# One over the sums on the values instead of the probabilities: eight blocks of attention instead of four

## The chip, the cores and the metric

The program runs on one core of one Trainium2 chip. A core has five engines, each with its own queue of instructions that it works through in order: TensorE (PE in the profile; PEld is its weight load) multiplies matrices, VectorE (DVE), ScalarE (ACT) and GpSimd (POOL) work element by element, and SyncE (SP) here only issues DMA transfers. The queues wait for each other by semaphores. What is measured is the time of one execution in microseconds (us). The median of three runs of the kernel before is 627.17 us (624.49, 627.32 and 627.17).

## The reference

Three layers follow one another. First comes an attention over q, k and v of 2 batches, 8 heads, 768 tokens and 64 features, in which a token sees itself, the 127 tokens before it and the first four of its batch:

```python
keep = is_sink | ((rel >= 0) & (rel < window))          # 4 sinks, window 128
scores = np.where(keep, scale * q @ k.T, -1e9)
a = np.exp(scores - scores.max(-1, keepdims=True))
a = a / (np.sum(a, axis=-1, keepdims=True) + 1e-09)
x = a @ v                                               # -> 1536 x 512
```

Then a gated layer, `silu(x @ w_gate) * (x @ w_val) @ w_out`, with weights of 512 x 1536 and 1536 x 512 that arrive as 64-bit floats. Last, a token with `x @ w_skip > 0` is sent to the one of eight experts that `x @ w_gate` ranks first, and the expert's `relu(x @ w1) @ w2`, times its probability, is added to x. The output is 1536 x 512 in float32.

## The kernel before

The 1536 tokens are 12 blocks of 128, six for each batch, and a block's eight heads are four pairs. Four blocks are a group (`GS = 4`). The gated layer takes the 1536 hidden columns in 12 chunks for one group at a time (`mlp(ph)`); a chunk is a projection with w_gate, one with w_val (`proj`, line 502) and, one chunk later, the product with w_out (`down`, line 514). All large products are made of three: high part times high part, high times low, low times high (`act_copy` makes a high part, `lo_of` subtracts it to get the low one; line 70 and line 73 are these two helpers).

The attention is a generator, `attention()`, that issues its work in pieces: `step_a` turns q and k of a pair (`tqk`), `step_b` makes the scores (`s`, line 296), applies the mask and finds the maximum on VectorE (line 312), and takes the exponential on ScalarE, which sums at the same time (line 316). `step_d` turns the probabilities (`tpt`, line 342), ScalarE copies them out (`pt`), and GpSimd zeroes what the mask excludes. `step_s` turns the probabilities of the sinks. `step_e`, once a block, multiplies the turned probabilities by the values (`xps`, lines 378 and 395) and splits the result into the high and low part `xt` that the projections read. Blocks 0 to 3 run alone; then the first pass of the gated layer begins (the first group, from about 67 to 208 us), and blocks 4 to 7 are issued in the gaps between its pieces, in proportion. Blocks 8 to 11 run in the second pass in the same way.

How the probabilities are divided by their sums depends on the block. For blocks below `LATE_SUM` the sums of all heads are kept in one tile (lines 305 to 308) and inverted once per block (line 325). In `step_e` eight matmuls spread the inverses into a PSUM tile `rps` (line 386: each takes one column of the inverses as a broadcast weight, against the unit matrix, 16 passes of 64 rows in the trace), ScalarE copies it to `rs` (line 388), VectorE multiplies the weighted values by it (line 401), and high and low part are made from the product. For the other blocks each pair inverts its two sums (lines 280 and 281), VectorE scales the probabilities of one head (line 323) and ScalarE those of the other (line 321).

While the first pass runs, its weights come in 36 pieces of 512 KB through three staging buffers (`st`). ScalarE and VectorE convert each piece in two instructions each (lines 136 and 137, then 141 and 142), and `prep` splits it into high part on ScalarE and low part on GpSimd (`ring`). In the same pass the rows of the experts' scratch in DRAM are cleared (`clear_rows`): eight transfers (line 602) from one zeroed tile (`trash`). That tile, `rs`, and some later tiles share one pool of four buffers (`"x2"`).

In PSUM, a pool of two buffers (`attp`) serves the attention of blocks 4 to 11: `tqk`, `s`, `tpt`, `tsk` and `xps` take turns in it. Another one of two (`gvp`) serves the projections, and for blocks 0 to 3 `tpt` and `rps`. Which instruction stands where on an engine's queue is set before the run by a scheduler that follows the order of issue, the priorities and when buffers come free.

Of the kernel before, what the change touches and what calls it, by code (L numbers as in the profile page):

```python
# [8 lines left out]
F32 = mybir.dt.float32  # L9
# [6 lines left out]
P = 128  # L16

@with_exitstack
def build(ctx: ExitStack, tc: tile.TileContext, q, k, v, n_sink, window,
# [5 lines left out]
    NPAIR = H // 2  # L25
# [6 lines left out]
    GS = 4  # L32
    FIRST = list(range(0, NB_ALL + 1, GS))
    GB = 2

    LATE_SUM = 4
    PHASES = [(0, 0, GS, 0, NFC, 2 * GS), (1, 0, GS, 0, NFC, 3 * GS)]
    PHASES += [(2, 0, GB, 0, NFC, 3 * GS), (2, GB, GS, 0, NFC, 3 * GS)]
    XT_SLOT = [0, 1, 0]
# [21 lines left out]
    gvp = fast.enter_context(tc.tile_pool(name="gvp", bufs=2, space=PSUM))  # L61
    attp = fast.enter_context(tc.tile_pool(name="attp", bufs=2, space=PSUM))
# [3 lines left out]
    att = early.enter_context(tc.tile_pool(name="att", bufs=1))  # L66
    sm = early.enter_context(tc.tile_pool(name="sm", bufs=2))

    def act_copy(out, in_, scale=1.0):
        nc.scalar.activation(out=out, in_=in_, func=ACTF.Copy, scale=scale)  # L70

    def lo_of(out, in_, hi, eng=None):
        (eng or nc.vector).tensor_tensor(out=out, in0=in_, in1=hi.bitcast(F32), op=ALU.subtract)  # L73
# [205 lines left out]
    def invert(s):  # L279
        nc.vector.tensor_scalar(out=s, in0=s, scalar1=1e-9, scalar2=None, op0=ALU.add)  # L280
        nc.vector.reciprocal(out=s, in_=s)

    def step_b(j):
# [20 lines left out]
        st = sm.tile([P, 4], F32, tag="st", name="st", bufs=3)  # L304
        if n < LATE_SUM:
            if pr == 0:
# [8 lines left out]
        for h in range(2):  # L315
            nc.scalar.activation(out=p[:, h], in_=p[:, h], func=ACTF.Exp, scale=-1.0, bias=st[:, h:h + 1], accum_out=su[:, h:h + 1])  # L316
        if n >= LATE_SUM:
            invert(su)
# [47 lines left out]
    def new_xt(slot, shape):  # L366
        return [xtp.tile(shape, F32R, tag=f"xt{a}{slot}", name=f"xt{a}") for a in range(2)]

    def step_e(n):

        b, i = divmod(n, NBLK)
        g = [n >= f for f in FIRST].index(False) - 1
        u = n - FIRST[g]
        x = (acqp if n < GS else attp).tile([P, NPAIR, P], F32, tag="acq" if n < GS else "att", name="xps")
        sk = skt.pop(n)

        for pr in range(NPAIR):
            nc.tensor.matmul(out=x[:, pr], lhsT=vsk[b][:, 2 * pr:2 * pr + 2, :].rearrange("p h d -> p (h d)"), rhs=sk,
                             start=pr == 0, stop=False, skip_group_check=True)
        if n < LATE_SUM:  # L380

            r = gvp.tile([P, NPAIR, P], F32, tag="gv", name="rps")
            inv = sums.pop(n)
            for pr in range(NPAIR):
                for h in range(2):
                    nc.tensor.matmul(out=r[64 * h:64 * h + 64, pr], lhsT=inv[:, 2 * pr + h:2 * pr + h + 1].to_broadcast([P, D]), rhs=ident, start=True, stop=True, skip_group_check=True)
            rs = mo.tile([P, RW], F32, tag="x2", name="rs", bufs=4)[:, 0:DM].rearrange("p (a f) -> p a f", a=NPAIR)
            act_copy(rs, r)
        last = 0 if i == 0 else 1
        for pr in range(NPAIR):  # L390
            d = pt.pop(NPAIR * n + pr)
            for s in range(last + 1):
                vv = vb[n - s]
                for h in range(2):
                    nc.tensor.matmul(out=x[64 * h:64 * h + 64, pr], lhsT=vv[:, 2 * pr + h, :], rhs=d[:, s, h],
                                     start=False, stop=s == last and pr == NPAIR - 1, skip_group_check=True)
        if u == 0:
            xt[g] = new_xt(XT_SLOT[g], [P, KD, NG])
        hi, lo = (xt[g][a][:, :, u * P:(u + 1) * P] for a in range(2))
        if n < LATE_SUM:  # L400
            nc.vector.tensor_tensor(out=rs, in0=x, in1=rs, op=ALU.mult)
            x = rs
        act_copy(hi, x)
        lo_of(lo, x, hi)
# [3 lines left out]
    def attention():  # L408
# [8 lines left out]
        for j in range(NP_ALL):  # L417
# [16 lines left out]
            if pr == 0 and n > 0 and n != GS:  # L434
                step_e(n - 1)
                done = n
                if n % NBLK == 0:
                    load_sinks(n // NBLK)
                yield done
            step_d(j)  # L440
            yield done
            if pr == NPAIR - 1:
                step_s(n)
                yield done
                if n == GS - 1:
                    step_e(n)
                    done = n + 1
                    yield done
        step_e(NB_ALL - 1)
        yield NB_ALL  # L450

# [801 lines left out]
```

## Time and profile before

| | |
|---|---|
| median of 3 runs | 627.17 us |
| profiled execution | 628.91 us, of which the span on the core is 627.2 |
| TensorE busy | 592.5 us (94%), mean granted clock 0.988 |
| VectorE busy | 443.4 us (71%) |
| ScalarE busy | 368.3 us (59%) |
| GpSimd busy | 192.1 us (31%) |

The profile is of one execution. TensorE is busy nearly the whole time, so what counts is where it is not, and what is added to its queue. "Busy" of TensorE is the time from the first to the last of its matmuls in flight. The granted clock is what share of full speed TensorE had. Idle time of another engine costs nothing by itself.

### The profile page before, as it was taken

Reading aid. Unit: us, or ns where it says so; the run is one execution under the profiler, and the core shown is the slowest. Engines: PE = TensorE matmul, PEld = TensorE weight load, DVE = VectorE, ACT = ScalarE, POOL = GpSimd, SP = SyncE. Lnnn points to the kernel's source line nnn. Section 1 sums busy time; section 2 is a strip of 40 time slices with the busy share of each in tenths; the row PEclk is TensorE's granted clock in tenths of the full one; section 3 lists DMA queues with packets and bytes.
Section 4 is the critical chain, followed back from the end, with each engine's and each line's share of the span. In section 5 each row is a group of like instructions: output and inputs, shape, how many; then the busy total and the mean of one; then the engine's idle time right before and its main releaser. Section 6 shows DMA issues by size and latency. Waiting matters only on the chain. (4 is left out here: it accounts for less than half of the span.)

```text
span 627.2 us, 10713 instructions
## 1 busy us (share of the span) xinstructions
PE 592.5 (94%) x3459; PEld 472.1 (75%) x3459; DVE 443.4 (71%) x1092; ACT 368.3 (59%) x863; POOL 192.1 (31%) x275
## 2 busy tenths in 40 slices
PE   5899998989999999999999999999998999999993
PEld 3566766667777878777778999899986777787772
DVE  3778889797546485665654577778748696989961
ACT  4699776876545355545543456657526675866740
POOL 2465352666343041101111030021005343526411
PEclk9999999989999999999999999999997999999998
DMA  8745879554010220100004200023107886968901
GB/s 201 166 142 154 244 243 271 184 169 101 1 34 1 85 52 18 33 15 4 1 1 152 101 30 2 0 67 111 36 35 229 284 262 212 331 210 286 322 9 38
DMA packets 78421, 75.83 MB, mean 121 GB/s; under 512 B 43138, under 2 KB 55426, under 8 KB 78352
## 3 DMA queue, kind: packets, MB, share of 16 engines
q1 hardware_dynamic: 75552, 69.32, 36.9%
q0 software_dynamic: 2512, 5.68, 2.7%
q8 instruction: 32, 0.52, 0.3%
q14 instruction: 37, 0.30, 0.2%
q10 hardware_dynamic: 288, 0.00, 0.0%
HBM read 65.37 MB, written 11.98 MB: 123 GB/s over the span
## 5 line engine op out<-in xcount | busy, mean ns | idle before, releaser
L502 PE MATMUL gv<-xt,ring 128*128 128x512 f32 (+1 forms) x1152 | 226.6, 346 | 0.4 <-DVE th L536 0.4
L502 PEld LDWEIGHTS gv<-xt,ring 128*128 128x128 f32 x1152 | 176.8, 190 | 27.4 <-issue 2.0
L70 ACT ACTIVATE ring<-w 128x512 fp32r<-128x512 f32 x144 | 90.2, 629 | 98.5 <-PE gv L502 72.1
L73 DVE TENSOR_TENSOR ring<-w,ring 128x512 fp32r<-128x512 f32 x108 | 74.6, 692 | 41.6 <-ACT ring L70 41.0
L514 PE MATMUL acc<-ring,hh 128*128 128x512 f32 x288 | 92.8, 402 | 1.0 <-POOL ring L73 0.6
L73 DVE TENSOR_TENSOR w<-stage,w 128x512 fp32r<-128x512 f32 x96 | 88.4, 954 | 6.9 <-ACT w L70 4.6
L70 ACT ACTIVATE w<-stage 128x512 fp32r<-128x512 f32 x128 | 73.0, 626 | 9.5 <-DMA stage<-in_moe_w_dram 5.5
L73 POOL TENSOR_TENSOR ring<-w,ring 128x512 fp32r<-128x512 f32 x36 | 50.0, 1391 | 53.9 <-ACT ring L70 48.5
L514 PEld LDWEIGHTS acc<-ring,hh 128*128 128x128 f32 x288 | 50.8, 188 | 12.8 <-POOL ring L73 1.0
L349 POOL TENSOR_SCALAR_AFFINE_SELECT pt<-pt 128x256 f32<-128x256 f32 x40 | 22.3, 557 | 124.4 <-ACT pt L70 124.4
L73 POOL TENSOR_TENSOR w<-stage,w 128x512 fp32r<-128x512 f32 x32 | 45.2, 1414 | 47.1 <-ACT w L70 25.1
L514 PE MATMUL acc<-ring,hl 128*128 128x512 f32 x144 | 57.3, 399 | 0.0
L316 ACT ACTIVATE p<-p,st 128x132 f32<-128x132 f32 x96 | 38.3, 400 | 29.7 <-DVE st L312 29.4
L924 PE MATMUL yps<-w,hT 128*128 128x512 f32 x192 | 47.1, 399 | 1.0 <-DVE w L73 0.6
L898 PE MATMUL hps<-w,xh 128*128 128x512 f32 x128 | 42.7, 413 | 0.8 <-issue 0.5
L924 PEld LDWEIGHTS yps<-w,hT 128*128 128x128 f32 x192 | 35.3, 188 | 10.4 <-ACTq L972 1.0
L296 PE MATMUL s<-kq 64*128 64x260 f32 (+1 forms) x144 | 38.3, 427 | 3.4 <-DVE st L312 1.6
L537 DVE TENSOR_TENSOR th<-th,gv 128x512 f32<-128x512 f32 (+1 forms) x48 | 26.5, 552 | 19.8 <-PE gv L502 17.6
L685 POOL DMA_INDIRECT xs<-x,pi x12 | 13.2, 1103 | 81.2 <-ACT ring L70 48.6
L70 ACT ACTIVATE hh<-th 128x512 fp32r<-128x512 f32 (+1 forms) x48 | 25.1, 523 | 17.9 <-DVE th L537 17.7
L296 PEld LDWEIGHTS s<-kq 64*128 64x128 f32 x144 | 18.4, 201 | 21.8 <-issue 13.8
L301 DVE COPY_PREDICATED s<-above,s 128x128 f32<-128x128 int32 x80 | 21.6, 290 | 18.5 <-PE s L296 18.2
(180 smaller groups left out, 951.2 us busy)
## 6 DMA issues: line engine op xcount, KB each, us to landing
stage<-in_moe_w_dram SPq DMA_DIRECT2D x128, 256.0 KB
st<-in_moe_w_gate_dram SPq DMA_DIRECT2D x12, 512.0 KB
st<-in_moe_w_val_dram SPq DMA_DIRECT2D x12, 512.0 KB
st<-in_moe_w_out_dram SPq DMA_DIRECT2D x12, 512.0 KB
xs<-trash SPq DMA_DIRECT2D x8, 387.0 KB
qk<-in_k_dram SPq DMA_DIRECT2D x12, 256.0 KB
qk<-in_q_dram SPq DMA_DIRECT2D x12, 256.0 KB
vb<-in_v_dram SPq DMA_DIRECT2D x12, 256.0 KB
```

The source lines that it names most:

```text
L70: nc.scalar.activation(out=out, in_=in_, func=ACTF.Copy, scale=scale)
L73: (eng or nc.vector).tensor_tensor(out=out, in0=in_, in1=hi.bitcast(F32), op=ALU.subtract)
L296: m_ = nc.tensor.matmul(out=ss[h][:, 0:nk], lhsT=x_, rhs=y_, start=m == 0, stop=m == len(terms) - 1)
L301: nc.vector.copy_predicated(ss[h][:, odd * W:odd * W + P], above, ss[h][:, (1 - odd) * W:(1 - odd) * W + P])
L316: nc.scalar.activation(out=p[:, h], in_=p[:, h], func=ACTF.Exp, scale=-1.0, bias=st[:, h:h + 1], accum_out=su[:, h:h + 1])
L349: nc.gpsimd.affine_select(out=d[:, 0], in_=d[:, 1], compare_op=ALU.is_ge, fill=0.0, base=0, pattern=[[0, 2], [1, P]], channel_multiplier=-1)
L502: nc.tensor.matmul(out=ps, lhsT=w_[:, kk * P:(kk + 1) * P], rhs=x_[:, kk, t0 * P:t1 * P], start=kk == 0 and m == 0, stop=kk == KD - 1 and ...
L514: nc.tensor.matmul(out=acc[g, t], lhsT=h_[:, s], rhs=w_, start=c == 0 and m == 0, stop=c == NFC - 1 and m == 2)
L537: nc.vector.tensor_tensor(out=th, in0=th, in1=vp, op=ALU.mult)
L685: d = nc.gpsimd.indirect_dma_start(out=xs[:, :], out_offset=bass.IndirectOffsetOnAxis(ap=pi[:, t], axis=0), in_=x2s[t], in_offset=None, bo ...
L898: nc.tensor.matmul(out=ps[half], lhsT=x_[:, kk, :], rhs=w_[:, kk, :], start=kk == 0 and m == 0, stop=kk == KD - 1 and m == 2)
L924: nc.tensor.matmul(out=y, lhsT=h_[:, c, :], rhs=w_[:, c % 4, :], start=c == 0 and m == 0, stop=c == NF2 - 1 and m == 2)
```

## The change

`LATE_SUM` goes from 4 to 8, so that blocks 4 to 7 too leave their probabilities as they are and multiply the weighted values. For these blocks the tile `rps` comes from the attention's own two PSUM buffers, not from those of the projections. Blocks 0 to 3 and 8 to 11 do the same work as before.

```diff
-    LATE_SUM = 4
+    LATE_SUM = 2 * GS
...
-            r = gvp.tile([P, NPAIR, P], F32, tag="gv", name="rps")
+            r = (gvp if n < GS else attp).tile([P, NPAIR, P], F32, tag="gv" if n < GS else "att", name="rps")
```

On TensorE, the `step_e` of block 4 (about 99 us in the trace before), between projections of the first group (`gv`). Before:

```order
L502 MATMUL gv<-xt_404,ring 128x512
L502 MATMUL gv<-xt_403,ring 128x512
L378 MATMUL xps<-skT,vs 128x128 x4
L395 MATMUL xps<-pt,vb 64x128 x16
L502 MATMUL gv<-xt_403,ring 128x512
```

And now:

```order
L502 MATMUL gv<-xt_404,ring 128x512
L502 MATMUL gv<-xt_403,ring 128x512
L378 MATMUL xps<-skT,vs 128x128 x4
L386 MATMUL rps<-ident,sums 64x128 x8
L395 MATMUL xps<-pt,vb 64x128 x16
L502 MATMUL gv<-xt_403,ring 128x512
```

The eight matmuls of the factors stand between the two kinds that make the weighted values; the same for blocks 5 to 7.

On ScalarE, what follows there (about 102 to 107 us in the trace before). `st` is a staged weight, `w32` the converted one, `xt0` the high part of block 4's values, `pt` and `kq` copies that free the attention's PSUM buffers. Before, with `st_1591` a piece of w_out and `st_1726` the next piece of w_gate:

```order
L136 ACTIVATE st_1591<-st_1591 128x512
L70 ACTIVATE xt0_1297<-xps_1276 128x4x128
L137 ACTIVATE w32_101<-st_1591 128x512
L136 ACTIVATE st_1726<-st_1726 128x512
L137 ACTIVATE w32_102<-st_1726 128x4x128
L70 ACTIVATE ring_106<-w32_100 128x512
L70 ACTIVATE pt_1345<-tpt_1342 128x256
L70 ACTIVATE kq03_250<-tqk_1349 128x256
```

And now, with `st_1717` that piece of w_gate and `st_1723` the next piece of w_val:

```order
L137 ACTIVATE w32_101<-st_1574 128x512
L70 ACTIVATE rs_1270<-rps_1261 128x512
L136 ACTIVATE st_1717<-st_1717 128x512
L137 ACTIVATE w32_102<-st_1717 128x4x128
L136 ACTIVATE st_1723<-st_1723 128x512
L70 ACTIVATE xt0_1288<-rs_1270 128x4x128
L137 ACTIVATE w32_103<-st_1723 128x4x128
L70 ACTIVATE ring_106<-w32_100 128x512
L70 ACTIVATE pt_1337<-tpt_1334 128x256
L70 ACTIVATE kq03_250<-tqk_1341 128x256
```

One more weight is converted ahead of the two copies at the end, and the high part is made later, since it now waits for VectorE's product.

On SyncE, the transfers of the same stretch. Before, `trash_1486` is sent between the weights from the first third of the pass on:

```order
L602 DMA xs_117<-trash_1486 96x2x516
L125 DMA st_1330<-in_moe_w_val_dram 128x4x256
L602 DMA xs_117<-trash_1486 96x2x516
L125 DMA st_1336<-in_moe_w_out_dram 128x1024
L602 DMA xs_117<-trash_1486 96x2x516
L125 DMA st_1444<-in_moe_w_gate_dram 128x4x256
```

Now the first of them stands behind that piece of w_val, ahead of values, keys and queries:

```order
L125 DMA st_1717<-in_moe_w_gate_dram 128x4x256
L125 DMA st_1723<-in_moe_w_val_dram 128x4x256
L602 DMA xs_117<-trash_1472 96x2x516
L81 DMA vb_1394<-in_v_dram 128x8x64
L602 DMA xs_117<-trash_1472 96x2x516
L81 DMA qk_1396<-in_k_dram 128x8x64
L81 DMA qk_1398<-in_q_dram 128x8x64
```

The first clearing transfer has moved from before the piece `st_1330` to eight weights later, because block 4's `rs` now takes its buffer of the shared pool ahead of `trash`.

## Rows read from the trace of the kernel before

**Rows 1.** Windows: busy us and instructions of each engine in four stretches.
```profile
core 0: us, PE busy (x) PEld busy (x) DVE busy (x) ACT busy (x) POOL busy (x), PEclk, DMA share, GB/s
67.00:100.00 33.00, 31.18 (x141) 22.60 (x142) 28.01 (x69) 25.09 (x61) 14.08 (x17) 1.00 0.85 249
100.00:133.00 33.00, 27.64 (x146) 20.22 (x143) 28.32 (x57) 24.87 (x57) 18.74 (x23) 0.97 0.73 214
133.00:208.00 75.00, 74.85 (x397) 57.61 (x398) 47.33 (x130) 42.37 (x110) 32.03 (x44) 0.99 0.17 45
131.30:134.70 3.40, 3.31 (x9) 2.74 (x10) 2.99 (x10) 2.61 (x8) 1.03 (x2) 0.51 0.64 186
```

**Rows 2.** Waits of TensorE, 67 to 208 us: total, times, longest (us).
```profile
PE tpt L342 <- DVE st L312: 4.1, 3, 2.2
PE s L296 <- ACT pt L70: 1.5, 1, 1.5
```

**Rows 3.** Groups by line, 67 to 208 us: busy us, mean ns of one.
```profile
L70 ACT ACTIVATE p<-p,st 128x132 f32<-128x132 f32 x15 | 6.0, 400 | 2.6 <-DVE st L281 2.6
...
L323 DVE TENSOR_SCALAR p<-p,st 128x132 f32<-128x132 f32 x15 | 5.4, 359 | 0.4
```

**Rows 4.** Timeline: start, duration (us), weight loads of the two kinds.
```profile
60.96 0.63 PEld L386 LDWEIGHTS rps<-ident,sums 128*64 128x64 f32 x10 [0.21 <-issue]
...
99.78 1.73 PEld L395 LDWEIGHTS xps<-pt,vb 128*64 128x64 f32 x32
```

**Rows 5.** Tile rs: durations in ns, least, median, most; first and last start.
```profile
L70 ACT ACTIVATE rs<-rps x4: 579/590/597, 27.1 to 62.7; 128x512 f32<-128x512 f32 x4
L401 DVE TENSOR_TENSOR rs<-xps,rs x4: 678/692/692, 29.8 to 65.8; 128x512 f32<-128x512 f32 x4
...
L73 DVE TENSOR_TENSOR xt<-rs,xt x4: 685/863/1280, 31.8 to 67.5; 128x512 fp32r<-128x512 f32 x4
```

**Rows 6.** Timeline at the end of the first pass.
```profile
210.26 0.69 DVE L73 TENSOR_TENSOR xt<-xps,xt 128x512 fp32r<-128x512 f32 x1 [0.71 <-ACT xt L70]
...
212.27 0.70 PE L502 MATMUL gv<-xt,ring 128*128 128x512 f32 x2
```

**Rows 7.** Timeline, 97 to 108 us: ScalarE, SyncE and TensorE.
```profile
97.65 0.69 ACT L136 ACTIVATE st<-st 128x512 int32<-128x512 uint16 x1 [1.69 <-DMA st<-in_moe_w_gate_dram]
...
99.89 0.37 SPq L125 DMA_DIRECT2D st<-in_moe_w_gate_dram  x1
...
103.65 0.37 SPq L125 DMA_DIRECT2D st<-in_moe_w_val_dram  x1
...
105.19 0.66 ACT L136 ACTIVATE st<-st 128x512 int32<-128x512 uint16 x1 [1.14 <-DMA st<-in_moe_w_gate_dram]
...
106.82 0.38 ACT L70 ACTIVATE pt<-tpt 128x256 f32<-128x256 f32 x1
...
107.26 0.97 PE L296 MATMUL s<-kq 64*128 64x260 f32 x4 [1.48 <-ACT pt L70]
```

**Rows 8.** Timeline, 86 to 90 us: ScalarE, VectorE and TensorE.
```profile
86.54 0.67 ACT L136 ACTIVATE st<-st 128x512 int32<-128x512 uint16 x1 [1.35 <-DMA st<-in_moe_w_out_dram]
...
87.24 0.69 DVE L141 SCALAR_TENSOR_TENSOR st<-st 128x512 int32<-128x512 int32 x1 [1.25 <-ACT st L136]
...
89.53 0.41 PE L342 MATMUL tpt<-ident,p 128*128 128x128 f32 x2 [1.23 <-DVE st L312]
```

**Rows 9.** Timeline, 126 to 132 us: GpSimd, VectorE and TensorE.
```profile
126.55 3.42 POOL L73 TENSOR_TENSOR ring<-w,ring 128x512 fp32r<-128x512 f32 x2
...
127.06 1.77 DVE L141 SCALAR_TENSOR_TENSOR st<-st 128x512 int32<-128x512 int32 x1
...
131.39 0.69 PE L342 MATMUL tpt<-ident,p 128*128 128x128 f32 x2 [2.22 <-DVE st L312]
```

**Rows 10.** Tile trash: durations in ns, first and last start in us.
```profile
L602 SPq DMA_DIRECT2D xs<-trash x8: 418/498/579, 71.6 to 118.5; - x8
```

**Rows 11.** DMA issues from 67 to 100 us: count, KB of each.
```profile
xs<-trash SPq DMA_DIRECT2D x5, 387.0 KB
```

## The prediction, made before the changed kernel ran

> **What bounds the kernel now.** The change reaches blocks 4 to 7 only, so I first cut the span into stretches, by busy time. In [rows 1] (67 to 208 us is the first expert layer's pass over blocks 0 to 3, in whose gaps blocks 4 to 7 of the attention run) TensorE is busy 74.85 of 75.00 us from 133 us on, and idle 1.82 and 5.36 us in the two stretches before. VectorE stands at 28 of 33 us there, DMA at 0.85 and 0.73. So in the later part whatever is put on TensorE's queue is paid in full, and whatever is taken off VectorE or ScalarE is worth nothing. In the earlier part the two engines are worth as much as they make TensorE wait. Second, the waits of TensorE in that part [rows 2]: of the 7.3 us idle in the three stretches, 4.1 are transposes of probabilities that wait until VectorE has read a score tile (they share two PSUM buffers), and 1.5 a score matmul behind ScalarE's copy of such a transpose; four smaller ones make up the rest. No wait is on the scaling of probabilities itself. Third, the rows around the longest waits, to see what stood in front.
>
> **What goes.** For 16 pairs of heads the two tiny instructions of the inversion, VectorE's scaling of one head and ScalarE's of the other: 16 times 0.36 and 16 times 0.40 us for the two scalings [rows 3], so 5.8 us of VectorE and 6.4 of ScalarE, and the inversions beside them. TensorE loses nothing. I cost all this at nothing by itself, since TensorE never waits for it; it counts below where it stood in the queue ahead of something waited for.
>
> **What comes, on TensorE.** Per block eight fp32 matmuls of 64 columns, 16 passes in the trace. Ten such passes took 0.63 us where the kernel has them now, after a gap of 0.21, and 32 passes of the same shape, those of the values, 1.73 us in a row [rows 4]. So 16 cost 0.87 by the second row and 1.0 plus the gap by the first: 3.5 to 4.9 us for four blocks. In the changed order they stand directly ahead of the value matmuls, so I take the neighbour's pace, rounded up: +3.6 us. Nothing lies over it.
>
> The rows show both kinds in the form 128*64. The Trainium skill, TensorEngine Tiling (Array Packing), section Key Properties, says that a change of tiling mode makes the engine drain first. By that rule the new place adds no change of mode and the low end holds; between two wide matmuls it would go towards the high end. No run here shows a drain alone.
>
> **What comes, elsewhere.** Per block an inversion of 8 columns, ScalarE's copy of the spread factors (0.59 us), and one VectorE multiplication of 0.69 [rows 5]. After it, high part and low part are made from SBUF. The rows for that already exist: the low part took 0.86 us in the middle and 1.28 at most [rows 5], against 0.69 when its input is PSUM [rows 6].
>
> The Trainium skill, SBUF — State Buffer, section Who interferes with whom, has a rule that speaks against the change: a VectorE instruction with two SBUF inputs contends with a GpSimd one that reads SBUF. The spread of 0.69 to 1.28 in rows 5 agrees with it. By the rule the last block's low part would be late by up to 0.6 us if GpSimd were reading then; GpSimd has no weights to split at that moment, so my sum leaves it out.
>
> **Where the waits go.** Four places.
> At 107.26 us a score matmul waits 1.48 us for a buffer that ScalarE's copy frees at 106.82; ScalarE had stood 1.14 us before a gate weight that DMA had not landed [rows 7]. In the changed order that weight still stands ahead of the copy, and so now does the next one, the value weight, with its two steps. In the trace its load is issued at 103.65, when VectorE has freed a staging buffer; the gate weight's took from 99.89 to 105.19, 5.3 us. With both as they are it lands at 108.95, and with the two steps of the conversion, the copy to the projection's input and a copy to the ring behind it, 0.6 each, the freeing copy runs at 111.35: 4.5 us later. But what came before is relieved: the conversion at 97.65 waited 1.69 us for its weight [rows 7] while clearing transfers ran (below), and ScalarE loses a scaling of 0.40. With both off, 2.1, it is 2.4 late; and if DMA is so much freer that no weight is late, the whole wait goes. I take the middle of -1.5 and +2.4: +0.5; bounds -1.5 and +4.5.
> At 89.53 a transpose waits 1.23 us, again behind a late weight (1.35 us at 86.54) [rows 8]. Now four more projection matmuls stand ahead of it, and fewer transfers compete (below). I take -1.0.
> At 131.39 a transpose waits 2.22 us for VectorE, which had a conversion step stretched to 1.77 us while GpSimd split weights [rows 9]. The changed order has four conversion steps instead of five ahead of it. One step is 0.69 undisturbed [rows 8] and 1.77 here: I take their middle, -1.2.
> Against that, near 116 us one of a pair's two transposes now stands ahead of six output matmuls that used to cover its wait for VectorE. Its price is the smallest wait of the kind, 4.1 less 1.23 and 2.22, which is 0.6: +0.6.
> Sum -1.1; bounds -5.6 (both rows of rows 2 gone) and +5.1 (4.5 and 0.6, with nothing gained).
> After the wait of 2.22, the granted clock is 0.51 for 3.4 us, the lower level, 1.2 GHz for 2.4, in which TensorE is busy 3.31 us [rows 1]. If the wait goes and the clock then stays up, half of that, 1.7 us, goes too. I leave half of that wait standing, so I take 0; bounds 0 and -1.7.
>
> **The end of the pass.** The low part for block 7 was ready at 210.95 and the first projection of the next pass ran at 212.27 [rows 6]: 1.3 us to spare. The chain gets one multiplication longer (0.69), and its high part now stands behind one more copy of finished sums on ScalarE (0.6, a copy of the size in rows 5). That uses the room up: +0.2; bounds 0 and +0.7.
>
> **A side effect in the queues.** The eight transfers that clear the expert rows (the first at 71.6, the last at 118.5 us [rows 10], five of them before 100 us, 387 KB each [rows 11]) come from a tile of the same four-buffer pool as the new factors. The factor of block 4 takes its buffer first, so the clearing tile is made after about 100 us, and the first transfer stands on SP's queue after eight more weight loads, right behind the value weight's load of above and ahead of a value and a query/key load. At 249 GB/s [rows 1] one takes 1.55 us. The early stretch loses this traffic, the one from 100 to 140 us gains it. I take 0 beyond what stands above; bounds -1.0 (one more early wait like that at 89.53 gone) and +1.5 (one late weight more, as in rows 7).
>
> **Sum.** 3.6 - 1.1 + 0.2 = +2.7 us. The profiled execution took 628.9 us (span 627.2, 1.7 around it), so 631.6 for such a one; the median of the runs shown is 627.2, so **629.9 us**. Nothing later changes: the rest of the program starts that much later.
>
> **Rivals.**
> Faster: the waits on the two shared buffers all go (-5.6), and the clock stays up (-1.7): with 3.6 for the matmuls -3.7, which is 623.5 us. For it: every one of these waits stands behind VectorE or ScalarE at 75 to 86% busy [rows 1], and these are what the change relieves, with DMA beside them. Against: even all sixteen scalings, 5.8 us, are little beside the 56 us of VectorE in the two stretches, and the waits stand behind weight conversions, which remain.
> Slower: the value weight is late at 107 us. ScalarE runs in order, so the copy that frees the shared buffer waits with it, the score matmul with the copy, and TensorE's queue with the matmul. At its full price of 4.5, and with only the 1.0 at 89.53 gained, 3.6 + 4.5 + 0.6 + 0.2 - 1.0 = +7.9, 635.1 us. For it: the order puts one conversion more ahead of the copy, and five clearing transfers move to behind that load, some 8 us of traffic (5 times 1.55), where DMA is at 0.73 already. Against: until then DMA is freer, and conversions come sooner. It decides once the weight lands later than about 105.3 on the old clock: the copy is then 0.9 later than before, and the sum passes 3.1.
> No effect: the matmuls fall where TensorE idles, and cost and gain are both nothing. In 133 to 208 us, where three of four blocks finish, there are 0.15 us of idle time, so I give this no chance of its own.
>
> **How the numbers follow.** The forecast gets 0.60, the faster rival 0.16, the slower 0.24. About 0.5% (3.1 us, 624.0 to 630.3) is what a measurement of this kernel can tell from no change. The forecast's own range is 626 to 632.5, since the wait at 107 alone moves it by 2 to either side; 0.42 of its chance lies within 630.3 and 0.18 above. So slower gets 0.18 + 0.24 = 0.42. The range leaves out a tenth on each side: most of the faster case lies above 623.5, most of the slower below 635.0.
>
> **What would show it.** In the profile after: 16 more passes of the factor matmuls per block, at 0.06 us each, directly ahead of those of the values; no scaling rows for 16 of 32 pairs; the waits at 89.5 and 131 gone or halved; the one at 107 still there, with ScalarE before a value weight, not a gate weight; the clearing transfers after 100 us; the next pass begun some 3 us after 212.3. If the wait at 107 is gone or the clock never falls, the faster rival gains; if it is over 4 us, the slower one. I would be wrong in the working if the factor matmuls cost over 1.3 us a block, or if a new wait for the two shared buffers stood at them.

## The result, and the profile after

The changed kernel takes 633.15 us in the median of 8 runs (630.31 to 636.38), the old one 627.80 in 8 runs beside them. The ratio is 1.0075, with a 95% interval from 1.0046 to 1.0105: slower by some 4.7 us (the medians lie 5.4 apart). Ratios here and below leave out executions more than 1.5% above the fastest of their kernel (three of seven in r10, one each in r4, r5 and r9, two of 29 of the old kernel beside r1 to r4); medians have all. Forecast were 629.9 us, and a difference below 3.1 us was given about the same chance as a loss above it. In the profiled executions the span grows by only 1.4 us (627.2 to 628.6), so the first task is to see by stages where time was lost and won. All stages come from the timelines: the start ends at the first projection of the first pass, the first pass at the first projection of the second, the middle at the first expert matmul, and the experts at the start of their last matmul.

| us | start | first pass | middle | experts | rest |
|---|---|---|---|---|---|
| before | 67.64 | 144.63 | 259.11 | 145.85 | 9.95 |
| after | 64.66 | 145.52 | 259.11 | 149.69 | 9.62 |

Three things stand in it. The start was 3 us shorter after. That is no effect of the change, as the order of work there is the same but for the last few instructions: the granted clock rises to its upper level at 22.0 us before and at 10.7 after. The first fence is of before, the second of after, both the timeline of the start (start, duration):

```profile
16.07 0.81 PE L296 MATMUL s<-kq 64*128 64x132 f32 x2
```

```profile
14.73 0.49 PE L296 MATMUL s<-kq 64*128 64x132 f32 x2
```

The same two score matmuls take 0.81 us in one and 0.49 in the other; the old kernel's second profile (below) has the short start too, 63.86 us. The first pass is 0.9 us longer, and the experts, which the change does not touch, 3.8.

The first pass after, by windows (columns as in [rows 1]):

```profile
67.00:100.00 33.00, 32.56 (x182) 24.77 (x181) 27.57 (x58) 25.86 (x57) 14.99 (x18) 1.00 0.69 212
100.00:133.00 33.00, 29.49 (x138) 21.35 (x138) 24.30 (x51) 22.46 (x53) 20.24 (x27) 1.00 0.80 241
133.00:208.00 75.00, 73.00 (x441) 56.66 (x440) 41.28 (x112) 39.65 (x100) 28.31 (x39) 1.00 0.16 39
```

And TensorE's waits in it, from 67 to 208 us (total, times, longest), beside [rows 2]:

```profile
PE s L296 <- ACT pt L70: 2.0, 1, 2.0
PE tpt L342 <- DVE st L312: 0.9, 2, 0.5
PE tpt L342 <- ACT rs L70: 0.8, 1, 0.8
PE acc L514 <- POOL ring L73: 0.6, 1, 0.6
PE s L296 <- DVE kq L73: 0.6, 1, 0.6
PE xps L378 <- DVE st L312: 0.6, 1, 0.6
PE tqk L265 <- DVE st L312: 0.4, 1, 0.4
```

TensorE is idle 0.44, 3.51 and 2.00 us where it was 1.82, 5.36 and 0.15 [rows 1] (the windows are the same on the clock, though the pass starts 3 us earlier after). The transposes' waits for VectorE fell from 4.1 to 0.9, the one at the score matmul grew from 1.5 to 2.0, and after 133 us, where there had been none, are new ones of 0.6 to 0.8. Between 100 and 133 us the granted clock is 1.00, where it fell to 0.51 after the old kernel's wait of 2.2 us.

The factor matmuls and the place of the score matmul, in the timeline after (answering to [rows 4, 7]):

```profile
94.87 1.09 PE L386 MATMUL rps<-ident,sums 128*64 128x128 f32 x16
95.79 1.92 PE L395 MATMUL xps<-pt,vb 128*64 128x128 f32 x32
...
101.17 0.67 ACT L136 ACTIVATE st<-st 128x512 int32<-128x512 uint16 x1 [1.17 <-DMA st<-in_moe_w_val_dram]
...
103.33 0.36 ACT L70 ACTIVATE pt<-tpt 128x256 f32<-128x256 f32 x1
...
103.75 0.48 PE L296 MATMUL s<-kq 64*128 64x260 f32 x1 [2.02 <-ACT pt L70]
```

The 16 passes take 0.92 us from their start to that of the values. ScalarE now waits for a value weight, and the copy behind it, and the score matmul behind that. The clearing transfers run from 98.2 to 125.0 us (before 71.6 to 118.5, [rows 10]):

```profile
L602 SPq DMA_DIRECT2D xs<-trash x8: 359/705/1570, 98.2 to 125.0; - x8
```

The experts: the first gather of their rows. Its rows were scattered into DRAM just before, by indirect transfers on GpSimd's queue, and the gather waits until they have landed. Before (timeline):

```profile
471.38 0.94 PE L898 MATMUL hps<-w,xh 128*128 128x512 f32 x3
471.38 0.99 POOL L685 DMA_INDIRECT xs<-x,pi  x1 [0.30 <-ACT xh L823]
...
474.36 2.12 SPq L796 DMA_DIRECT2D xg<-xs  x4
...
478.17 0.46 PE L839 MATMUL xgt<-ident,xg 64*128 64x64 f32 x4 [0.96 <-DMA xg<-xs]
```

After:

```profile
469.28 0.94 PE L898 MATMUL hps<-w,xh 128*128 128x512 f32 x3
469.28 0.98 POOL L685 DMA_INDIRECT xs<-x,pi  x1 [0.30 <-ACT xh L823]
...
474.17 2.12 SPq L796 DMA_DIRECT2D xg<-xs  x4
...
479.27 0.68 PE L839 MATMUL xgt<-ident,xg 64*128 64x64 f32 x4 [4.14 <-DMA xg<-xs]
```

With the last scatter and the first expert matmul issued in the same instant, the gather is issued 2.98 us later before, and 4.89 after; TensorE waits 0.96 and 4.14 us for its rows. The scatter's landing time is why, by the DMA view of both (issues from 1.3 us before that instant; the last number is us to landing). Before, and after:

```profile
xs<-x,pi POOLq DMA_INDIRECT x2, 3.0
```

```profile
xs<-x,pi POOLq DMA_INDIRECT x2, 4.9
```

Why does the same scatter land later? The DMA view from 1.0 to 4.5 us after that instant (first row: share of the DMA engines busy in 40 slices, in tenths; then queue, kind, packets, MB, share). Before:

```profile
DMA  0000009797989500000000000000000006118697
...
q0 software_dynamic: 86, 0.26, 19.4%
q1 hardware_dynamic: 46, 0.09, 12.3%
```

After:

```profile
DMA  0000009797979400000000000030000200101000
...
q0 software_dynamic: 86, 0.26, 20.0%
q8 instruction: 1, 0.02, 3.0%
```

The scatter (q0) has the same 86 packets in both. Before, it is through after the first block of nines, and the gather (q1) follows. After, five single packets of it come straggling from 3.3 to 4.35 us (the 3, 2, 1 and 1; the fifth is too short to show), and one transfer of another kind lies in the stretch: 16 KB of instructions (q8), which takes 1.7 us, from 1.62 to 3.32. The first late packet starts at 3.31, and each of the others as the one before it ends. Such transfers come all through the run, mostly 15 to 30 us apart. Around the first expert matmul, before has them at -5.9 and +17.0 us, after at +1.6. The change puts 64 more passes on TensorE's queue ahead of this point. So a theory was to be tested (theory 5 in the expectations below; theory 6 is its rival): code for TensorE is loaded in pieces while it runs, 64 more passes moved one piece onto the scatter, and the last rows of the scatter waited behind it.

### The profile page after: what moved, and what is told of

Its sections match the earlier page's. It is cut to its first block, busy times and chain, and to the rows that moved or that the text cites. A ratio compares the mean times of both kernels' runs of the same rounds, so it can differ in the third digit from the quotient of the medians.

```text
span 628.6 us, 10789 instructions
## 1 busy us (share of the span) xinstructions
PE 591.5 (94%) x3523; PEld 472.9 (75%) x3523; DVE 435.5 (69%) x1056; ACT 365.1 (58%) x851; POOL 192.4 (31%) x275
## 5 line engine op out<-in xcount | busy, mean ns | idle before, releaser
L296 PE MATMUL s<-kq 64*128 64x260 f32 (+1 forms) x144 | 36.5, 404 | 4.5 <-ACT pt L70 2.3
```

The source lines that it names most:

```text
L296: m_ = nc.tensor.matmul(out=ss[h][:, 0:nk], lhsT=x_, rhs=y_, start=m == 0, stop=m == len(terms) - 1)
```

## The experiments

Medians are of 12 timed runs, 7 where so stated and 6 for the fourth and ninth; the old kernel beside them stood at 627.0 to 628.0. The runs of one kernel spread over some 5 to 10 us, and the ratios' intervals reach some 2 us to either side, so that a difference of medians below 2 us says little. The stages of the profiles are finer, but they too differ between executions of one program: the first pass of the old kernel is 144.63, 143.81 and 142.44 us in three (r6 does the same work until then). This table gathers them: first pass, place of the 16 KB code transfer nearest the scatter (us after the first expert matmul), longest wait of TensorE for gathered rows, the experts' part, and how long the granted clock was at its lower level (0.50) in the first pass and in the 20 us after the first expert matmul.

| kernel | median | first pass | code at | wait | experts | low, pass | low, experts |
|---|---|---|---|---|---|---|---|
| old (profile above) | 627.80 | 144.63 | -5.9 | 1.3 | 145.85 | 3.4 | 6.8 |
| old again (r11) | | 143.81 | -5.6 | 1.0 | 145.72 | 3.4 | 6.8 |
| old, clearing late (r3) | 629.56 | 145.71 | -6.1 | 0.9 | 145.54 | 3.4 | 3.4 |
| old, 64 tiny passes (r6) | 628.34 | 142.44 | +1.7 | none | 144.79 | 3.4 | 3.4 |
| changed (profile above) | 633.15 | 145.52 | +1.6 | 4.1 | 149.69 | 0 | 10.2 |
| changed again (r1) | 632.52 | 144.76 | +2.4 | 3.9 | 147.99 | 0 | 6.8 |
| changed, clearing early (r2) | 629.34 | 145.91 | +1.3 | 3.8 | 147.57 | 3.4 | 6.8 |
| the same again (r12) | 630.02 | 144.61 | +1.4 | 3.3 | 148.67 | 3.4 | 10.2 |
| changed, code moved (r5) | 630.18 | 146.68 | -2.6 | 0.9 | 145.98 | 3.4 | 6.8 |
| both (r7) | 631.25 | 144.60 | -2.6 | 2.9 | 149.04 | 3.4 | 10.2 |
| old, factor matmuls only (r8) | 633.68 | 146.96 | +2.1 | 3.7 | 149.11 | 3.4 | 10.2 |
| half the factor matmuls (r9) | 634.72 | 149.42 | -6.0 | 0.8 | 146.98 | 13.7 | 6.8 |

**The changed kernel again** (r1), no edit.

> The changed kernel once more, unchanged, for a second profile. In the first pair of profiles the span grew by 1.4 us only, while the medians differ by 5: the old one's clock rose late at the start (3.3 us lost before 20 us), and its experts' part (first expert matmul to last) took 145.9 us against 149.7. Theory 1 (the cost lies in the first pass, start and experts differ by chance): first pass, first projection of it to first of the next, again 145.5 +- 0.7 us (old 144.6); experts anywhere between 145 and 150. Theory 2 (the change also slows the experts' part): experts again at 149 or more. Median 632 to 634 in both.

Measured: 632.52 us, ratio 1.0072 (1.0034 to 1.0109), first pass 144.76, experts 147.99, with the same late gather. So the experts' loss was no chance of one profile, although it stays short of the 149 that was named for theory 2.

**Clearing early** (r2, r12).

```diff
-    def clear_rows():
+    def clear_rows(trash):
...
                 make_routing_consts()
-                rows = clear_rows()
+                trash = mo.tile([P, RW], F32, tag="x2", name="trash", bufs=4)
+                make_trash(trash)
+                rows = clear_rows(trash)
```

> The changed kernel with the clearing tile made before block 4 takes its factor buffer, so that the eight clearing transfers run early again, as in the old kernel. Theory 1 (factor matmuls on TensorE's queue set the cost): within 1 us of the changed kernel, about 632 to 633. Theory 3 (the displaced transfers delay weights): the wait near 104 us (2.0 us behind the copy of probabilities) goes or falls under 0.7, first pass 1.5 to 3 us shorter, median 630 to 631.

> The changed kernel with the clearing transfers early, once more. Its first median was 3.2 us below the changed kernel's, but its profile had no shorter first pass (145.9 us against 144.8 to 146.7) and the same late gather; with the code transfer moved off the scatter, early clearing gained nothing (631.3 against 630.2). If the displaced transfers cost 3 us: 629 to 630 again, and a first pass under 145. If the first median was chance: 632 to 633, first pass 145 to 147, gather wait 4 us.

Measured: 629.34 and 630.02, ratios to the old kernel 1.0034 (1.0005 to 1.0063) and 1.0027 (0.9997 to 1.0058). The times are 2.5 to 3.8 us below the changed kernel's, both times, and the gather is as late. TensorE's waits in the first pass of r2:

```profile
PE tpt L342 <- DVE st L312: 3.1, 3, 2.4
...
PE s L296 <- ACT pt L70: 0.5, 1, 0.5
```

The wait behind the copy of probabilities is 0.5 us (none of it is left in r12), where the changed kernel has 1.5 to 2.0: that sign of theory 3 came true. But a transpose again waits 2.4 us for VectorE, as in the old kernel, and behind it the granted clock falls for 3.4 us in r2, r12 and r7 alike. In the changed order this wait is 0.5. So it is the moved clearing, with what it displaces, that took this wait away and lengthened the other. In sum the first pass is hardly shorter. The times speak for theory 3; the profiles show the wait that went, but not a gain of 3 us.

**The old kernel with the clearing late** (r3).

```diff
+        if n == GS:
+            begun["lo4"] = lo
...
         make_trash(trash)
+        nc.gpsimd.tensor_scalar(out=trash[:, 0:1], in0=begun["lo4"].bitcast(F32)[:, 0, 0:1], scalar1=0.0, scalar2=None, op0=ALU.mult)
```

(`lo4` is the low part of block 4's values.)

> The old kernel, with the clearing tile made to depend on block 4's values, so that the clearing transfers run late as in the changed one. Nothing else changes. Theory 1: same as the old kernel, 627 to 629. Theory 3: 2 to 3 us slower than the old one, 630 to 631, with a longer wait for a weight on ScalarE between 100 and 120 us.

Measured: 629.56, ratio 1.0053 (1.0023 to 1.0084), first pass 145.71 against 142.44 to 144.63. Slower, by 1.6 in the medians and 3.3 by the ratio, if less than the 630 to 631 that was named. The transfers alone are not shown to cost this: the added instruction stood 3.65 us at the head of GpSimd's queue until block 4's values were there, and what is behind it there came later too. Waits of TensorE in the first pass:

```profile
PE s L296 <- DVE kq L73: 2.6, 1, 2.6
PE tpt L342 <- DVE st L312: 2.3, 2, 1.7
PE tqk L265 <- DVE xt L73: 1.2, 1, 1.2
PE tqk L265 <- ACT pt L70: 0.6, 1, 0.6
```

They stand at other places than those in [rows 2], and these four sum to 6.7 us.

**No factors for blocks 4 to 7** (r4).

```diff
-        if n < LATE_SUM:
+        if n < GS:
             r = ...
-        if n < LATE_SUM:
+        if n < GS:
             nc.vector.tensor_tensor(out=rs, in0=x, in1=rs, op=ALU.mult)
```

> The changed kernel without the factors for blocks 4 to 7: no factor matmuls, no copy of them and no multiplication, so these blocks' values stay undivided by the sums (this part of the computation is left out). What is left of the change is what it removes. Theory 1: the first pass is shorter than in the changed kernel by the matmuls, 3.6 us, and the waits that they add, so 141 to 142 us, median 627 to 629.5. Theory 4 (the matmuls fill gaps and the cost lies in new waits from another order): within 1.5 us of the changed kernel.

Measured: a first pass of 139.65 us, below the 141 to 142 that was named. With undivided values tokens go to other experts, so what comes after says nothing here, nor does the total of 666.5. The pass in windows:

```profile
63.80:100.00 36.20, 35.28 (x181) 26.08 (x181) 29.15 (x67) 28.41 (x64) 14.88 (x17) 1.00 0.90 267
100.00:133.00 33.00, 29.43 (x140) 21.51 (x140) 28.01 (x56) 25.16 (x57) 20.62 (x27) 1.00 0.68 210
133.00:203.50 70.50, 70.50 (x401) 54.95 (x400) 36.20 (x104) 37.52 (x98) 27.85 (x39) 1.00 0.15 36
```

What the change removes makes the pass 2.8 to 5.0 us shorter than the three old ones: no fall of the clock, and an idle time of 4.5 instead of 5.5 to 7.3. What it adds makes it 5.1 to 7.0 us longer again: 3.7 for the passes (4 times 0.92), the rest in waits and, in r5, in the clock, with the last 70 us no longer free of waits. The clearing is early in r4 (from 70.3 us), so what it costs to displace it is in this too.

**The code transfer moved** (r5).

```diff
-        filler(10)
-        warm(4, acqp, "acq")
+        filler(8)
+        tiny = acqp.tile([P, 512], F32, tag="acq", name="tiny")
+        for _ in range(32):
+            nc.tensor.matmul(out=tiny[0:32, 0:8], lhsT=idle[:, 0:32], rhs=idle[:, 0:8], start=True, stop=True)
```

> The changed kernel, and just before the experts, where TensorE waits for the routing, 6 of its idle matmuls replaced by 32 tiny ones (8 columns): 26 passes, 52 instructions more on TensorE's queue; the order on all other engines is the same. In the three profiles with blocks 0 to 7 on factors, the first gather of expert rows comes 2.9 us later after the first expert matmul than in the two with blocks 0 to 3, and a 16 KB transfer of the instruction queue runs at 1.5 to 2 us after that matmul, in the middle of the scatter that the gather waits for (in the other two 5.9 us before it). Theory 5 (64 more passes moved that code transfer onto the scatter): it moves about 6 us earlier, the wait for the first gathered rows falls from 4 to about 1 us, the experts' part to 145.5 to 146.5 us, median about 3 us below the changed kernel, 629.5 to 630.5. Theory 6 (buffers or rows of the changed kernel make the gather late): wait still 4 us, median 632 to 634.

Measured: 630.18, ratio 1.0038 (1.0001 to 1.0074), within the named range and 2.3 to 3.0 below the changed kernel. The transfer is at -2.6 (4 us earlier, where 6 were expected), experts 145.98, and the scatter and the gather are back to the old times (timeline, and landing):

```profile
473.95 0.98 POOL L685 DMA_INDIRECT xs<-x,pi  x1 [0.30 <-ACT xh L825]
...
476.84 2.12 SPq L798 DMA_DIRECT2D xg<-xs  x4
...
480.52 0.46 PE L841 MATMUL xgt<-ident,xg 64*128 64x64 f32 x4 [0.75 <-DMA xg<-xs]
```

```profile
xs<-x,pi POOLq DMA_INDIRECT x2, 2.9
```

The gather is issued 2.89 us after the last scatter, as before the change. The edit is on TensorE's queue alone, and only the 16 KB transfer (q8) moved; the nearest one of 8 KB (q14) is at -1.0 in this profile as in r1. Theory 6 falls.

**64 tiny passes more in the old kernel** (r6): the same edit with 2 for the fillers and 76 for the tiny matmuls.

> The old kernel with 76 tiny matmuls in place of 12 idle ones at the same point: 64 passes more on TensorE's queue, as many as the factors of four blocks, but in an idle place. Theory 5: the code transfer falls on the scatter, the wait for the first gathered rows is 3.5 to 4.5 us, experts 148 to 149.5, median 2.5 to 5 us above the old kernel (up to 2 of it for the tiny matmuls themselves). Theory 6: wait about 1 us, experts 145 to 146, median at most 2 us above the old one.

Measured: 628.34, ratio 1.0014 (0.9982 to 1.0047), experts 144.79. By the numbers that were named this goes to theory 6, but the aim was missed. The tiny matmuls held the first expert matmul up by 2.4 us, the scatter did not wait for them (its last packet ends 0.87 us after that matmul), and the gather was issued 1.4 us after it, so the code transfer at +1.7 came when the scatter was through. A wait of 4 us was expected for theory 5 and is not there, nor was the transfer on the scatter; so it tests neither.

**Factor matmuls only** (r8): the old kernel, and in blocks 4 to 7 eight matmuls whose result is not read.

```diff
+        elif n < 2 * GS:
+            r = attp.tile([P, NPAIR, P], F32, tag="att", name="rps")
+            for pr in range(NPAIR):
+                for h in range(2):
+                    nc.tensor.matmul(out=r[64 * h:64 * h + 64, pr], lhsT=ident[:, 2 * pr + h:2 * pr + h + 1].to_broadcast([P, D]), rhs=ident, start=True, stop=True, skip_group_check=True)
```

> The old kernel plus the eight factor matmuls a block for blocks 4 to 7, whose result nobody reads; everything else as before. Forecast's sum: first pass longer by the matmuls, 3.5 to 4.9 us, and with theory 5 the experts longer by 2.9 too, since these are the same 64 passes: 633 to 636. Rival (they fall into waits): first pass longer by under 1.5 us.

Measured: 633.68 (7 runs), ratio 1.0090 (1.0055 to 1.0124), first pass 146.96, 2.3 to 4.5 above the old one (3.3 above the mean of three), experts 149.11, and this in TensorE's waits for the experts:

```profile
PE xgt L844 <- DMA xg<-xs: 4.6, 2, 3.7
```

In a kernel with the old values and the old clearing, 64 passes (and the turn that their tile takes in the attention's two PSUM buffers) bring the late gather with them. This is the test from the other side that r6 was to be. It alone makes the old kernel as slow as the changed one.

**Both cures** (r7): the edits of r2 and r5.

> The changed kernel with both: clearing transfers early again and the code transfer moved off the scatter. If the two together are what the change costs, 626 to 628, no slower than the old kernel; if the factor matmuls cost 3 us by themselves, 629 or more.

Measured: 631.25, ratio 1.0037 (1.0008 to 1.0066): above 629, and no better than r5. Here an 8 KB transfer of the other instruction queue ran 2.4 us after the first expert matmul, and TensorE waited 1.7 and 2.9 us for the first and the second gather. So moving one piece of code let another come near, and the gather was late again (experts 149.04): whether both cures together are worth more than one, r7 can't say. Its first pass is 2.1 us shorter than r5's, with one fall of the clock in each.

**Half the factor matmuls** (r9, r10).

```diff
+            nc.gpsimd.tensor_copy(rs.rearrange("p a (h d) -> p a h d", h=2), inv.rearrange("p (a h) -> p a h", a=NPAIR).unsqueeze(3).to_broadcast([P, NPAIR, 2, D]))
             for pr in range(NPAIR):
-                for h in range(2):
-                    nc.tensor.matmul(out=r[64 * h:64 * h + 64, pr], ...
+                nc.tensor.matmul(out=r[:, pr], lhsT=rs[:, pr], rhs=ident, start=True, stop=True)
```

> The changed kernel with half the factor matmuls in all eight blocks: GpSimd spreads the inverses over 64 columns each in the tile of the factors, and four matmuls of 128 columns take the place of eight of 64. TensorE then has as many passes in all as in the old kernel. Theory 5 (the code transfer on the scatter, 64 passes on the queue) with the forecast's price of the matmuls: the code transfer is back near 6 us before the first expert matmul, the wait for the first gathered rows about 1 us, experts 145.5 to 146.5 us, the first pass 1.8 us shorter than in the changed kernel (that one 144.8 to 146.7), median 627 to 629. If the gather is late for another reason: wait 4 us, 630.5 to 632.

> The same with the clearing transfers early, as in the old kernel. If the displaced transfers cost what the two medians of 632.5 and 629.3 say (3 us), 625 to 627, faster than the old kernel; if that difference was chance and the start's clock, the same as the one before, 627 to 629.

Measured: 634.72 and 635.96 (7 runs), ratios 1.0120 (1.0068 to 1.0173) and 1.0126 (1.0071 to 1.0180), neither better than the changed kernel. As many passes as in the old kernel do bring the code transfer to -6.0 and the wait to 0.8. But the first pass is 149.42 us: the new order has waits of 3.5 and 2.9 us for the shared buffers there, and the granted clock is 0.94 and 0.90 in its first two stretches.

```profile
PE s L296 <- ACT kq L70: 3.5, 1, 3.5
PE s L296 <- ACT pt L70: 2.9, 1, 2.9
```

The clock stands at its lower level for 13.7 us of that pass, and half of this, 6.8, is more than the pass is longer. So this is no better version; the saving of 1.8 us that was expected is lost several times over to the rearranged queue.

**The old kernel again** (r11), no edit, one execution.

> The old kernel once more, for a second profile of its first pass. By the forecast it is 2 to 3 us shorter than the changed kernel's (144.8, 145.5 and 146.7 in three profiles): 142.5 to 144.6 us, and experts 145 to 146.5.

Measured: first pass 143.81, experts 145.72, both as named, start 63.86; 624.24 us. Its clock falls at the same place of the pass as in the first profile; the mean of these 4 us is 0.58 (windows):

```profile
127.00:131.00 4.00, 4.00 (x15) 3.17 (x13) 2.78 (x7) 2.68 (x9) 1.03 (x2) 0.58 0.72 233
```

## Why the prediction held in its range, and which step failed

The forecast of +2.7 us was made for the first pass (of the gated layer, which the prediction once calls the first expert layer). Three profiles of the changed order (145.52, 144.76, and 146.68 in r5) against three of the old one (144.63, 143.81, and 142.44 in r6) give a mean of 145.65 against 143.63: +2.0. By terms it is 3.7 for the passes, 0.8 less idle time of TensorE in the whole pass (5.7 against 6.5 on the mean; forecast 1.1 less), and 1.1 less for the clock.

- **Factor matmuls, +3.6.** 0.92 us a block from start to start, 3.7 in all. Alone, in r8, they lengthen the pass by 3.3 on the mean; TensorE's idle time there is 6.4, as in the old kernel, so they did not fall into waits.
- **The score matmul behind the value weight, +0.5.** 2.0 us for 1.5, with ScalarE 1.17 us before the value weight: mechanism and size as forecast. With the clearing early (r2, r12, r7) it is 0.5 at most, so this wait belongs to the moved clearing.
- **The transposes.** The one at 89.53 waits no longer (-1.2, forecast -1.0), the one at 131 waits 0.5 (-1.7, forecast -1.2), the third, 0.6 at 109.5, is gone, which was not forecast, and the split pair near 116 waits 0.4 (forecast +0.6). The reason given for the one at 131 holds, four conversion steps ahead of it for five; but it is the moved clearing that brings this, not the scalings that went: in r2 there are five again, and the wait is 2.4.
- **Missed in the pass.** New waits after 133 us: 0.8 behind the copy of the factors, which takes its turn in the two shared buffers, and two of 0.6. The prediction named a wait at the factors as a sign against it; it is there. On the other side the clock stays up in two of the three profiles, which I had left at 0 with a bound of -1.7; half of the 3.4 us at the lower level is what that gives each time. In r5 it falls for 3.4 us at 107.6, just after the score matmul's wait of 1.9, and that pass is the longest of the three.
- **The end of the pass.** From the last projection of the first pass to the first of the next are 10.08 us before and 10.94 after. The difference is about that of the passes of block 7's factors, 0.92; nothing of the +0.2 for a longer chain is to be seen.
- **What I costed at nothing.** Taking the scalings out shortens the pass by 4.0 us on the mean (r4), of which 2.0 is idle time and 1.7 the clock; I gave 1.1 net to the waits. It is not seen whole in the total, since the factors, and the clearing that they displace, bring waits of their own.
- **The step that failed**: "Nothing later changes: the rest of the program starts that much later." Mean experts' part, changed: 148.8 (149.69 and 147.99), old: 145.8 (145.85 and 145.72), so +3.0, more than the whole forecast. It begins with one wait, for the scatter's landing at the first gather. That 64 passes suffice for it is shown by r8, that moving the code transfer undoes it by r5, and that it goes with the 64 passes by r9. In the six profiles with late packets (after, r1, r2, r7, r8, r12) the first one starts within 0.02 us of the end of a code transfer; in the eight others no code transfer runs while the scatter's packets do, and none of these is late. So the late packets ran behind the code; what the two share, the trace does not name.

The clock adds to the wait. The 20 us from the first expert matmul on (windows; the third number from the end is the granted clock), first r1, then after:

```profile
471.05:491.05 20.00, 14.12 (x62) 10.64 (x60) 14.70 (x21) 11.98 (x23) 9.20 (x10) 0.83 0.80 252
```

```profile
469.28:489.28 20.00, 14.66 (x60) 11.34 (x59) 15.19 (x21) 12.00 (x23) 8.62 (x10) 0.74 0.80 252
```

A mean of 0.83 is 6.8 us at the lower level, as in both old profiles, and 0.74 is 10.2 us. At 6.8 the experts are 2.2 us longer than the old ones (r1); the after profile, at 10.2, is 1.7 longer still, half of the 3.4 us more. Every profile at 10.2 has the late gather, but not the other way round (r1, r2); what decides between the two is open.

2.0 and 3.0 make 5.0, and the rest of the program gives back 0.3; measured were 4.7, between 2.9 and 6.6. That the time fell into the wide range (623.5 to 635.0) was luck: it lies above the forecast's own range of 626 to 632.5, and the room above that had been left for other misfortunes of this size in the first pass. The rival that was to make it slower, a late value weight at its full price of 4.5, did not happen: that wait is 2.0.

Open is the clearing. Late clearing, with an instruction that also holds GpSimd up, slows the old kernel by 1.6 to 3.3 us, and its first pass is 1.1 to 3.3 longer. Early clearing makes the changed kernel faster by some 3 us in two sets of runs, but three profiles with it (145.91, 144.61, 144.60) show only 0.6 in the pass. One reason is the clock: it falls in all three, and in only one of the three with the clearing late. Against that one (r5, 146.68) they are 0.8 to 2.1 shorter. My bound of +1.5 for this side effect may have been too narrow; the runs don't settle it.

## What to carry to other kernels

When a change adds or removes instructions on an engine, look past its stage: the places where code is loaded shift for what follows (here a transfer came 1.6 us after the first expert matmul, where the nearest had been 5.9 before and 17.0 after it), and a chain that waits for one small transfer (scatter, then gather) is where that is paid. A difference in a stage that the change doesn't touch is to be compared over several profiles before it is called chance. And on a queue that is full, take the work that is added at its full price, and count what the removal frees as waits only after both orders have been seen.

## What was not expected of the hardware

- A 16 KB instruction transfer of 1.0 to 1.7 us beside a scatter (two issues, 0.52 MB) goes with a landing of the second issue that is later: 4.9 us after against 3.0 before, 4.3 in r8, and 2.9 where it was moved away (r5). One of 8 KB and 0.3 us does it too (3.7 in r7).
- After the first gather, executions of one program stood at the lower clock for 6.8 us (r1) or for 10.2 (after), and the experts' part differed by 1.7 us.
- The same program starts in 64 or in 67.6 us, by how long TensorE stays at the lower level there (0.81 us against 0.49 for the same two matmuls): the granted clock rises at 10.9 or 22.0 us in the old kernel (63.86 and 67.64), at 10.7 in the changed one (64.66), and in r1 it rises at 10.1, falls at 13.5 and rises again at 20.3 (67.17). That is 3 of the 5 to 10 us by which single runs differ.
